# Laying r and k out with tokens along the row in a fused linear-attention and adapter-mixture kernel

## The chip, the cores and the metric

The kernel runs on one core of a Trainium2 chip. Five engines work side by side and meet at semaphores: TensorE (PE; its weight loads are listed as PEld), VectorE (DVE), ScalarE (ACT), GpSimd (POOL) and SyncE (SP, which here only issues DMAs). Matrix products land in PSUM, eight banks of 2 KB per partition; everything else lives in SBUF. The metric is the device time of one launch in microseconds, as a median over runs.

## The reference

Four batches of eight heads are run through a recurrence over 768 tokens with head size 48. Its output, seen as 3072 tokens of width 384, goes through a mixture of eight rank-16 adapters, of which each token takes the two with the largest gate logits.

```python
for t in range(S):                      # r, k, v, w: (4, 8, 768, 48); u: (8, 48)
    cur = np.einsum('bhd,bhe->bhde', u[None] * kt, vt)
    y[:, :, t] = np.einsum('bhd,bhde->bhe', rt, state + cur)
    state = wt[:, :, :, None] * state + np.einsum('bhd,bhe->bhde', kt, vt)
...
logits = x @ w_gate                     # x: y as (3072, 384)
topk = np.argpartition(-logits, K, axis=1)[:, :K]       # K = 2
...                                     # w: softmax over the two selected logits
delta[mask] += w[mask, k, None] * ((x[mask] @ A[e]) @ B[e])
return x + delta
```

## The kernel before, in words

The 3072 tokens are 24 tiles (`t`) of 128 tokens, six tiles per batch. A tile holds all eight heads, as four pairs `p` of two heads `g`, and everything below is done once per tile unless said otherwise.

- **Loads.** SP loads w (`load_w`) and v (`load_v`) in groups of one to three tiles, and r and k of one tile in one transfer (`load_rk`, 384 KB, eight buffers), all as f32 with tokens on the partitions and heads times 48 channels along the row. u and the adapter weights (`moe`) are loaded once.
- **Decay.** ACT takes the logarithm of w per group (`ln`). TensorE sums it over the tokens of the tile, and of the tile before, by triangular matrices into the bank `cs_ps`, in two steps: `csr` gives the sum before a token (it scales r), `csk` adds the token's own term (it scales k). ACT takes the exponentials (`expr`, `expk`) one after the other into a single bank `e_ps`, and DVE multiplies them onto r and k (`multr`, `multk`) into the bf16 tile `rk2`.
- **Turn.** TensorE transposes the eight 128-wide blocks of `rk2` (`trr`, `trk`) into `trp`, and ACT on even tiles, DVE on odd ones, copies them out (`trev`), so that channels are on the partitions.
- **Attention inside the tile.** TensorE multiplies turned k by turned r per head (`amm`, into `a_ps`, two banks); DVE applies the triangular mask to all 1024 columns at once (`aev`).
- **State.** TensorE accumulates k times v into the bank `s_ps` (`kv`), and ACT copies the sum to SBUF (`sev`). v comes as bf16 from a cast on ACT, per group (`vcast`).
- **Bonus, the u term.** POOL multiplies r by k (`rkk`) and by u (`rku`), DVE sums over the channels of each head (`diag`), POOL multiplies v by it (`dv`).
- **Output.** TensorE adds into `y_ps` the state's part and the bonus (`yin`) and the attention's part (`yat`); ACT copies it to SBUF (`xTev`).
- **Adapters.** TensorE computes logits into the same bank `s_ps` (`lg`); small instructions on ACT, DVE and POOL find the two largest (`lgs`, `gmax`, `gsel`, `gsub`, `gexp`, `gmul`, `gden`, `gnorm`); `zmm`, `zw`, `zT`, `zTev` apply A and the gate for three tiles at a time (one at the very end); `dx` and `dmm` add x and the product with B; ACT copies the result (`oev`) and SP stores it.

PSUM is handed out by name: one bank each for `cs_ps`, `s_ps`, `e_ps`, `trp`, `y_ps`, two for `a_ps`, and one (`m`) for the adapters, which near the end also borrow banks that are no longer used (`Z_BANK`, `D_BANK`).

The order of work is fixed: `ORDER` is one written list of task names, and each engine runs its own tasks in the order of that list. A planner class (`Plan`) holds the dependences and can make such a list from costs and priorities, but with `ORDER` present it only looks the tasks up. So an engine whose next task waits does not take a later one. Dependences that the list does not spell out are enforced by the framework, which adds the waits: two instructions that touch the same PSUM bank are kept in the order in which they are written.

Of the kernel before, what the change touches and what calls it, by code (L numbers as in the profile page):

```python
# [8 lines left out]
F32 = mybir.dt.float32  # L9
# [8 lines left out]
CENTRE = 52.0  # L18
# [5 lines left out]
    ld_u=-990.0,  # L24
    ld_v0=-985.0,
    ld_w1=-980.0,
    ld_rk1=-975.0,
    ld_rk2=-970.0,
    ld_v1=-965.0,
    ld_w2=-960.0,  # L30
    ld_rk3=-955.0,
    ld_rk4=-950.0,
    ld_rk5=-945.0,
    ld_v2=-940.0,
    ld_moe=-935.0,
    ld_w3=-930.0,
    ld_rk6=-925.0,
    ld_rk7=-920.0,
    ld_rk8=-915.0,
    ld_v3=-910.0,  # L40
    ld_w4=-905.0,
    ld_rk9=-900.0,
    ld_rk10=-895.0,
    ld_rk11=-890.0,
    ld_v4=-885.0,
    ld_w5=-880.0,
    ld_rk12=-875.0,
    ld_rk13=-870.0,
    ld_rk14=-865.0,
    ld_v5=-860.0,  # L50
    ld_w6=-855.0,
    ld_rk15=-850.0,
    ld_rk16=-845.0,
    ld_rk17=-840.0,
    ld_v6=-835.0,
    ld_w7=-830.0,
    ld_rk18=-825.0,
    ld_rk19=-820.0,
    ld_rk20=-815.0,
    ld_v7=-810.0,  # L60
    ld_w8=-805.0,
    ld_rk21=-800.0,
    ld_rk22=-795.0,
    ld_rk23=-790.0,
    ld_v8=-785.0,
    ln=17.78,
    csr=6.47,
    expr=-0.97,
    csk=0.14,
    multr=-14.6,  # L70
    expk=-5.95,
    multk=-9.66,
    rkk=10.33,
    rku=1.66,
    diag=6.67,
    dv=10.4,
    vcast=10.01,
    trr=13.31,
    trk=-10.55,
    trev=0.12,  # L80
    amm=10.34,
    aev=6.22,
    kv=-2.45,
    sev=11.79,
    yin=28.6,
    yat=-8.86,
    xTev=11.98,
    lg=15.76,
    dmm=8.44,
    oev=-6.55,  # L90
    store=0.0,
    lgs=5.8,
    gmax=-6.24,
    gsub=-4.6,
    gsel=-5.0,
    dx=5.0,
    gexp=5.87,
    gmul=7.19,
    gden=8.29,
    gnorm=-1.8,  # L100
    zmm=3.51,
    zw=-8.82,
    zT=-3.52,
    zTev=9.05,
# [11 lines left out]
consts ld_w0 ld_rk0 ln0 csr0 ld_v0 expr0 rkk0 ld_w1 csk0 multr0 vcast0 expk0 trr0 ld_u multk0 ln1 ld_rk1 kv0 rku0  # L116
csr1 trk0 sev0 expr1 ld_rk2 rkk1 trev0 csk1 multr1 diag0 ld_v1 expk1 amm0 csr2 trr1 multk1 rku1 dv0 rkk2 trk1 aev0
ld_w2 expr2 vcast1 yin0 csk2 multr2 trev1 rku2 expk2 kv1 yat0 ld_rk3 ln2 diag1 amm1 trr2 csr3 diag2 multk2 dv1
ld_rk4 aev1 sev1 xTev0 trk2 rkk3 expr3 ld_rk5 trev2 yin1 csk3 kv2 rku3 multr3 expk3 yat1 trr3 amm2 ld_v2 xTev1 diag3
multk3 csr4 dv2 rkk4 aev2 sev2 expr4 ld_moe rku4 rkk5 yin2 trk3 csk4 yat2 multr4 vcast2 trev3 expk4 ld_w3 kv3 xTev2  # L120
cast_wg multk4 dv3 rku5 sev3 trr4 csr5 diag4 trk4 expr5 amm3 trev4 multr5 ld_rk6 csk5 kv4 aev3 dv4 yin3 trr5 expk5
ln3 ld_rk7 rkk6 amm4 diag5 multk5 yat3 cast_A csr6 ld_rk8 aev4 xTev3 lg0 trk5 expr6 yin4 rku6 rkk7 dv5 cast_B ld_v3
multr6 csk6 trev5 expk6 sev4 lg1 yat4 xTev4 multk6 lg2 csr7 lg3 amm5 lg4 trr6 diag6 ld_w4 expr7 vcast3 rku7 rkk8
aev5 multr7 trk6 yin5 csk7 kv6 trev6 rku8 dv6 ld_rk9 yat5 diag7 expk7 amm6 ld_rk10 xTev5 multk7 rkk9 sev6 aev6 csr8
lg5 expr8 kv7 trr7 ld_rk11 lgs0 ln4 sev7 trk7 rkk10 gmax0 csk8 yin6 multr8 yat6 ld_v4 gsub0 gsel0 trev7 rku9 expk8
gexp0 csr9 multk8 xTev6 trr8 gmul0 diag8 dv7 expr9 trk8 ld_w5 gden0 trev8 amm7 kv8 lg6 multr9 gnorm0 csk9 yin7 aev7
expk9 sev8 zmm0 vcast4 dv8 rkk11 ld_rk12 multk9 csr10 zw0 yat7 amm8 expr10 diag9 ld_rk13 zT0 csk10 kv9 multr10 xTev7
rku10 rku11 dv9 rkk12 zTev0 yin8 trr9 trk9 expk10 aev8 ld_rk14 dmm0 ln5 csr11 multk10 ld_v5 oev0 yat8 trev9 sev9
expr11 dmm1 rku12 diag10 lg7 trr10 csk11 oev1 multr11 xTev8 ld_w6 diag11 expk11 trk10 dmm2 lg8 amm9 diag12 oev2
csr12 multk11 dv10 rkk13 dv11 trev10 aev9 ld_rk15 expr12 vcast5 multr12 zmm3 yin9 csk12 amm10 ld_rk16 zw3 yat9  # L130
expk12 aev10 rku13 rkk14 rku14 kv10 trr11 zT3 xTev9 ld_rk17 sev10 ln6 trk11 csr13 yin10 multk12 trev11 ld_v6 yat10
expr13 diag13 trr12 xTev10 trk12 diag14 rkk15 amm11 lg9 lg10 csk13 trev12 multr13 aev11 kv12 yin11 trr13 dv12 rku15
expk13 ld_w7 vcast6 csr14 multk13 yat11 zTev3 diag15 expr14 amm12 multr14 store2 ld_rk18 dmm3 trk13 csk14 xTev11
sev12 aev12 oev3 expk14 ld_rk19 store3 rkk16 dv13 rkk17 rku16 lg11 yin12 kv13 dmm4 csr15 multk14 yat12 trev13
ld_rk20 diag16 trr14 lgs1 ln7 expr15 sev13 multr15 xTev12 rku17 rkk18 amm13 csk15 trk14 gmax1 oev4 kv14 lg12 expk15
ld_v7 store4 gsub1 trev14 dv14 dmm5 yin13 csr16 gsel1 aev13 multk15 gexp1 yat13 sev14 diag17 gmul1 expr16 ld_w8 dv15
gden1 xTev13 amm14 trr15 trk15 csk16 kv15 multr16 oev5 gnorm1 lg13 yin14 aev14 dv16 rkk19 expk16 sev15 vcast7 zmm6
rku18 dv17 rkk20 multk16 ld_rk21 csr17 trev15 expr17 zw6 kv16 yat14 amm15 ld_rk22 multr17 csk17 zT6 trr16 trk16
# [725 lines left out]
```

## Time and profile before

| | |
|---|---|
| median of 3 runs | 102.93 us (102.78 to 103.38) |
| the profiled execution | 103.02 us, of which the span of the profile is 101.3 us |
| busy: PE, DVE, ACT, POOL | 85.6, 85.2, 80.5, 69.8 us (84%, 84%, 79%, 69% of the span) |
| weight loads (PEld) | 60.7 us |
| DMA | 24.5 MB, 9809 packets; the queue's packets took 64.5% of the 16 engines' span |
| granted TensorE clock | 0.989 of full speed |

Durations are those of one profiled execution. Records overlap: eight matmuls of L460 have 222 ns each and are over in 0.40 us, and on DVE a mask multiplication recorded with 1.22 us is followed by the next instruction after 1.13 us. Where the time that an instruction holds its engine is wanted, the chain of waits is read, in which pieces follow one another without overlap.

### The profile page before, as it was taken

How to read it: one execution, taken by the hardware profiler on the slowest of the kernel's cores; microseconds unless marked ns; L12 is line 12 of the kernel's file. 1: busy time of each engine (PE TensorE's matmuls, PEld its weight loads, DVE VectorE, ACT ScalarE, POOL GpSimd, SP SyncE). 2: the span in 40 equal slices, each digit the busy share in tenths (PEclk: the TensorE clock that was granted, in tenths of full speed). 3: DMA queues.
4: the chain of work that ended last, by engine and by line, in shares of the span. 5: the costliest groups of instructions: out<-in, count | busy, mean ns of one | idle time of the engine just before them, and what ended most of it. 6: DMA issues, size and time to landing. Idle time of an engine off the chain costs nothing.

```text
span 101.3 us, 3568 instructions
## 1 busy us (share of the span) xinstructions
PE 85.6 (84%) x1400; PEld 60.7 (60%) x1400; DVE 85.2 (84%) x203; ACT 80.5 (79%) x160; POOL 69.8 (69%) x93
## 2 busy tenths in 40 slices
PE   1238899998698699999999999999988999999930
PEld 0014556566476477677766686678765777778620
DVE  4723898989978899999999899899969898988920
ACT  5347589999699898999999898798995678764640
POOL 6317989999999889999999989999972400000000
PEclk9999999999999999999999999999999999999995
DMA  2899999999999976948006989961224003224173
GB/s 55 298 312 400 414 421 422 409 417 413 428 398 422 416 258 209 385 149 283 11 0 194 377 283 312 382 250 66 100 82 154 6 32 126 84 78 155 40 292 140
DMA packets 9809, 24.50 MB, mean 242 GB/s; under 512 B 1088, under 2 KB 4544, under 8 KB 9792
## 3 DMA queue, kind: packets, MB, share of 16 engines
q1 hardware_dynamic: 9792, 24.27, 64.5%
q8 instruction: 11, 0.18, 0.7%
q14 instruction: 6, 0.05, 0.1%
HBM read 19.55 MB, written 4.72 MB: 240 GB/s over the span
## 4 chain that ended last, share of the span: by engine, by line
PE 54%; DVE 22%; ACT 7%; DMA 5%; issue 4%; POOL 3%; SPq 1%; ACTq 1%; DVEq 0%
DVE at L466 8%; PE y_ps L508 6%; PE a_ps L460 6%; PE y_ps L499 5%; PE y_ps L494 5%; DMA v_in<-in_v_dram 5%; PE trp L438 4%; PE z_ps L601 4%; PE d_ps L640 4%; PE trp L443 3%; DVE rk L414 3%; DVE rkT L449 3%; PE s_ps L476 3%; PE cs_ps L388 3%; PE s_ps L519 3%
## 5 line engine op out<-in xcount | busy, mean ns | idle before, releaser
L466 DVE TENSOR_TENSOR at<-a_ps,at_mask 128x1024 bf16<-128x1024 f32 x24 | 29.3, 1219 | 1.4 <-PE a_ps L460 1.3
L422 POOL TENSOR_TENSOR rku<-rku,u_sb 128x384 f32<-128x384 f32 x24 | 23.9, 1000 | 3.4 <-DMA u_sb<-in_u_dram 2.6
L418 POOL TENSOR_TENSOR rku<-rk_in 128x384 f32<-128x384 f32 x24 | 23.9, 998 | 1.7 <-DMA rk_in<-in_rk_dram 1.7
L431 POOL TENSOR_TENSOR dv<-v_in,diag 128x384 bf16<-128x384 f32 x24 | 19.8, 830 | 0.2 <-DVE diag L426 0.2
L514 ACT CAST xT<-y_ps 128x512 bf16<-128x512 f32 x24 | 14.3, 598 | 2.0 <-PE y_ps L508 1.9
L398 ACT ACTIVATE e_ps<-cs_ps 128x384 f32<-128x384 f32 x24 | 11.7, 486 | 5.1 <-PE cs_ps L390 2.5
L409 DVE TENSOR_TENSOR rk<-rk_in,e_ps 128x384 bf16<-128x384 f32 x24 | 13.2, 548 | 2.9 <-ACT e_ps L398 2.9
L414 DVE TENSOR_TENSOR rk<-rk_in,e_ps 128x384 bf16<-128x384 f32 x24 | 13.2, 549 | 2.6 <-ACT e_ps L403 2.5
L403 ACT ACTIVATE e_ps<-cs_ps 128x384 f32<-128x384 f32 x24 | 11.8, 493 | 2.2 <-PE cs_ps L393 1.2
L426 DVE TENSOR_REDUCE diag<-rku 128x8 f32<-128x384 f32 x24 | 12.8, 548 | 0.3 <-POOL rku L422 0.3
L651 ACT COPY res<-d_ps 128x384 f32<-128x384 f32 x22 | 10.6, 486 | 2.6 <-PE d_ps L647 2.1
L451 ACT COPY rkT<-trp 128x1024 bf16<-128x1024 bf16 x12 | 12.3, 1026 | 0.0
L379 ACT CAST v_bf<-v_in 128x1152 bf16<-128x1152 f32 (+2 forms) x9 | 9.4, 1048 | 1.6 <-DMA v_in<-in_v_dram 1.6
L438 PE MATMUL trp<-ident,rk 128*128 128x128 bf16 x96 | 9.8, 227 | 1.0 <-DVE rkT L449 0.7
L373 ACT ACTIVATE logw<-w_in 128x1152 f16<-128x1152 f32 (+2 forms) x9 | 9.6, 1061 | 1.3 <-DMA w_in<-in_w_dram 1.2
L460 PE MATMUL a_ps<-rkT 48*128 48x128 bf16 x192 | 9.8, 222 | 0.9 <-ACT rkT L451 0.7
L390 PE MATMUL cs_ps<-logw,strict 128*128 128x384 f16 x24 | 8.4, 349 | 2.1 <-ACT logw L373 2.1
L508 PE MATMUL y_ps<-at,v_bf 128*64 128x128 bf16 x192 | 9.8, 224 | 0.2
L443 PE MATMUL trp<-ident,rk 128*128 128x128 bf16 x96 | 9.8, 227 | 0.1
L499 PE MATMUL y_ps<-ident,dv 128*128 128x128 bf16 x96 | 9.7, 225 | 0.0
L438 PEld LDWEIGHTS <-rk 128*128 128x128 bf16 x96 | 6.5, 101 | 4.3 <-DVE rk L409 1.5
L393 PE MATMUL cs_ps<-logw,ident 128*128 128x384 f16 x24 | 8.3, 348 | 0.7 <-ACT e_ps L398 0.6
(71 smaller groups left out, 160.8 us busy)
## 6 DMA issues: line engine op xcount, KB each, us to landing
rk_in<-in_rk_dram SPq DMA_DIRECT2D x24, 384.0 KB, 7.2
out_dram<-res SPq DMA_DIRECT2D x24, 192.0 KB, 1.9
w_in<-in_w_dram SPq DMA_DIRECT2D x7, 576.0 KB, 8.3
v_in<-in_v_dram SPq DMA_DIRECT2D x7, 576.0 KB, 8.4
moe_f<-in_moe_dram SPq DMA_DIRECT2D x1, 464.0 KB, 8.7
w_in<-in_w_dram SPq DMA_DIRECT2D x1, 384.0 KB, 5.2
v_in<-in_v_dram SPq DMA_DIRECT2D x1, 384.0 KB, 6.9
w_in<-in_w_dram SPq DMA_DIRECT2D x1, 192.0 KB, 2.4
```

The costliest lines, as they stand in the source:

```text
L409: nc.vector.tensor_mul(rk2[:, 0].rearrange("s p h d -> s (p h) d")[:, :, 0:D], chunk(t, "r"), st[t]["er"])
L414: nc.vector.tensor_mul(rk2[:, 1].rearrange("s p h d -> s (p h) d")[:, :, 0:D], chunk(t, "k"), st[t]["ek"])
L418: nc.gpsimd.tensor_mul(rku, chunk(t, "r"), chunk(t, "k"))
L422: nc.gpsimd.tensor_mul(st[t]["rku"], st[t]["rku"], u_sb)
L431: nc.gpsimd.tensor_mul(dv_[:, :, 0:D], chunk(t, "v"), st[t]["diag"].to_broadcast([L, H, D]))
L438: nc.tensor.transpose(trp[:, 0, p, :], st[t]["rk2"][:, 0, p, :, :].rearrange("s a b -> s (a b)"), ident)
L443: nc.tensor.transpose(st[t]["trp"][:, 1, p, :], st[t]["rk2"][:, 1, p, :, :].rearrange("s a b -> s (a b)"), ident)
L460: nc.tensor.matmul(a_ps[:, g, p, :], lhsT=rkT[base:base + D, 1, p, :], rhs=rkT[base:base + D, 0, p, :], start=True, stop=True)
L466: nc.vector.tensor_mul(at, st[t]["a_ps"].rearrange("s g p f -> s (g p) f"), at_mask.to_broadcast([128, H, 128]))
L499: nc.tensor.matmul(y_ps[:, p, :], lhsT=dv_[:, 2 * p:2 * p + 2, :].rearrange("s a b -> s (a b)"), rhs=ident, start=(c == 0 and p == 0), sto ...
L508: nc.tensor.matmul(y_ps[g * 64:(g + 1) * 64, p, :], lhsT=vb[:, 2 * p + g, :], rhs=at[:, g * P + p, :], start=False, stop=(p == P - 1), ski ...
L514: nc.scalar.copy(out=xT_, in_=st[t]["y_ps"])
```

## The change

r and k come from the host with channels on the partitions and tokens along the row (head pairs padded from 48 to 64 channels, so a tile is 512 KB; after the eight buffers have been filled once, 112 of 128 partitions, 448 KB). The log sums are made in that shape, with logw as the stationary operand and the triangular matrix moving, once per tile (`cs`) in place of the two steps; the sum before a token is the sum up to the token before it, so r is multiplied by the exponential shifted by one column (`multr`) and its first column by the last column of the tile before (`rz`). Scaled r and k are then already turned: `trr`, `trk`, `trev` are gone, and only k is transposed back for the state (`ktr`, `knev`; not in the last tile of a batch). The constant that centres the exponents moves from a matmul into the bias of the exponentials. The bonus is one product on POOL and a sum on TensorE against a block form of u (`rkk`, `bon`, into a further part of `s_ps`), copied out by ACT (`diag`). v is padded to 64 per head on the host and cast to bf16 by its DMA, which POOL issues; so are the adapter weights with u. `vcast`, the three `cast_` tasks, `rku` and the load of u are gone. `aev` is two instructions, one per bank. Except for `cs_ps` and `s_ps`, PSUM is one pool of six banks: a task that takes a bank gets the one that has been free longest in the written order. `ORDER` is written anew, with `PRIO` and the planner's costs.

The parts of the diff that do the work (`PRIO`, `ORDER`, the planner's costs and the removed functions, which stand above, are left out):

```diff
     def load_v(gi):
-        nc.sync.dma_start(out=g["v"][:, 0:g["n"]], in_=v[:, g["t0"]:g["t0"] + g["n"]])
+        g["v"] = ld.tile([L, GN, H, DP], BF16, name="v_bf", bufs=NV)
+        nc.gpsimd.dma_start(out=g["v"][:, 0:g["n"]], in_=v[:, g["t0"]:g["t0"] + g["n"]])
     def load_rk(t):
+        st[t]["rk"] = rk_ins[t % NRKI]
+        rows = 128 if t < NRKI else 64 + D
+        nc.sync.dma_start(out=st[t]["rk"][0:rows], in_=rk[0:rows, t])
+    def load_moe():
+        nc.gpsimd.dma_start(out=moe_bf, in_=moe)
...
+    def bank(key, shape, dt):
+        taken[key] = idle.pop(0)
+        return pp.tile(shape, dt, name=f"bk{taken[key]}", tag=f"bk{taken[key]}")
+    def release(key):
+        idle.append(taken.pop(key))
...
+    def cs(t):
         c = t % NC
+        for p in range(P):
+            if c > 0:
+                nc.tensor.matmul(cs_ps[:, p, :], lhsT=pair_of(grp(t - 1, "logw"), p), rhs=rest, start=False,
+                                 stop=False, skip_group_check=True)
+            nc.tensor.matmul(cs_ps[:, p, :], lhsT=pair_of(grp(t, "logw"), p), rhs=incl, start=(c == 0 and p == 0),
+                             stop=True, skip_group_check=True)
+    def expr(t):
+        e = bank(f"er{t}", [128, P, 128], F32)
+        nc.scalar.activation(out=e, in_=cs_ps, func=ACT.Exp, bias=up)
+    def expk(t):
+        e = bank(f"ek{t}", [128, P, 128], F32)
+        nc.scalar.activation(out=e, in_=cs_ps, func=ACT.Exp, bias=down, scale=-1.0)
+    def multr(t):
+        nc.vector.tensor_mul(st[t]["rT"][:, :, 1:128], st[t]["rk"][:, 0, :, 1:128], st[t]["er"][:, :, 0:127])
+    def rz(t):
+        if t % NC == 0:
+            nc.gpsimd.memset(rTs[t % NRT][:, :, 0:1], 0.0)
         else:
+            nc.vector.tensor_mul(rTs[t % NRT][:, :, 0:1], st[t]["rk"][:, 0, :, 0:1], st[t - 1]["er"][:, :, 127:128])
     def multk(t):
+        nc.vector.tensor_mul(st[t]["kT"], st[t]["rk"][:, 1], st[t]["ek"])
     def rkk(t):
+        x = wk.tile([128, P, 128], BF16, name="rkx", bufs=3)
+        nc.gpsimd.tensor_mul(x, st[t]["rk"][:, 0], st[t]["rk"][:, 1])
+    def bon(t):
+        for p in range(P):
+            nc.tensor.matmul(dg_ps[:, t % NSL, :], lhsT=st[t]["rkx"][:, p, :], rhs=u_bf[:, p, :],
+                             start=False, stop=(p == P - 1), skip_group_check=True)
     def diag(t):
-        nc.vector.tensor_reduce(out=dg, in_=st[t]["rku"], axis=AX.X, op=ALU.add)
+        nc.scalar.copy(out=dg.rearrange("s h o -> s (h o)"), in_=dg_ps[:, t % NSL, :])
+    def ktr(t):
+        kn_ps = bank(f"kn{t}", [L, P, 128], BF16)
         for p in range(P):
+            nc.tensor.transpose(kn_ps[:, p, :], st[t]["kT"][:, p, :], ident)
+    def knev(t):
+        x = st[t]["kn_ps"].rearrange("s p (g d) -> s (p g) d", g=2)[:, :, 0:D]
+        if knev_on_dve(t):                                # odd tiles
+            nc.vector.tensor_copy(out=kn, in_=x)
         else:
+            nc.scalar.copy(out=kn, in_=x)
+    def amm(t, g):                                        # one bank per call, all eight matmuls in the second
+        st[t]["a_ps", g] = bank(f"a{g}_{t}", [128, P, 128], F32)
...
+    def aev(t, i):
+        at = wk.tile([128, 4, 128], BF16, name=f"at{i}")
+        nc.vector.tensor_mul(at, st[t]["a_ps", i], at_mask.to_broadcast([128, 4, 128]))
```

The new list begins so:

```
consts ld_moe ld_w0 ld_rk0 ln0 cs0 ld_w1 expk0 rkk0 expr0 multk0 ld_rk1 ln1 multr0 rz0 ld_v0 bon0 ktr0 diag0 cs1
ld_rk2 knev0 rz1 amma0 ammb0 rkk1 expk1 aevb0 expr1 ld_w2 multk1 cs2 rkk2 multr1 ktr1 expk2 bon1 aeva0 diag1 expr2
dv0 bon2 ld_rk3 rz2 amma1 ln2 kv0 ammb1 ld_v1 knev1 multk2 yin0 multr2 yat0 ld_rk4 sev0 cs3 rz3 diag2 aevb1 rkk3
```

## The prediction, made before the changed kernel was run

> **What bounds the kernel now.** I read the busy shares by stage first.
>
> ```profile
> 10.00:35.00 25.00, 21.28 (x336) 14.62 (x335) 22.63 (x43) 21.91 (x43) 24.11 (x29) 1.00 1.03 416
> 35.00:62.00 27.00, 26.59 (x476) 19.21 (x476) 26.54 (x54) 25.95 (x51) 25.68 (x32) 1.00 0.67 224
> 62.00:95.00 33.00, 31.73 (x552) 23.84 (x547) 29.86 (x76) 25.00 (x53) 15.19 (x20) 1.00 0.35 128
> ```
>
> The columns are the stretch, then busy us of PE, PEld, DVE, ACT and POOL, the clock, the DMA share and GB/s. No engine is alone at its limit: POOL is full up to 35 us (24.11 of 25), PE and DVE are at 98% up to 62 us, and afterwards PE leads (31.73 of 33) while POOL runs dry. DMA is full only in the first stretch. Then the chain that ended last, by engine:
>
> ```profile
> PE 54%; DVE 22%; ACT 7%; DMA 5%; issue 4%; POOL 3%; SPq 1%; ACTq 1%; DVEq 0%
> ```
>
> So PE sets 54.7 us of the 101.3 and DVE 22.3. The same chain in order of time shows what an instruction holds its engine when the next stands right behind it (start, length):
>
> ```profile
> 56.66 1.13 DVE at L466
> 57.79 0.46 DVE rk L414
> 58.25 0.46 DVE diag L426
> ...
> 68.11 0.33 PE a_ps L460 x8
> 68.44 0.33 PE trp L438 x4
> 69.10 0.22 PE trp L443 x4
> ```
>
> 1024 columns hold DVE 1.13 us and 384 hold it 0.46, which is 1.05 ns a column; four 128-wide transposes with their weight loads hold PE 0.22. For ACT and POOL I use the costliest groups (busy, mean ns, idle before):
>
> ```profile
> L422 POOL TENSOR_TENSOR rku<-rku,u_sb 128x384 f32<-128x384 f32 x24 | 23.9, 1000 | 3.4 <-DMA u_sb<-in_u_dram 2.6
> L418 POOL TENSOR_TENSOR rku<-rk_in 128x384 f32<-128x384 f32 x24 | 23.9, 998 | 1.7 <-DMA rk_in<-in_rk_dram 1.7
> L514 ACT CAST xT<-y_ps 128x512 bf16<-128x512 f32 x24 | 14.3, 598 | 2.0 <-PE y_ps L508 1.9
> L451 ACT COPY rkT<-trp 128x1024 bf16<-128x1024 bf16 x12 | 12.3, 1026 | 0.0
> L379 ACT CAST v_bf<-v_in 128x1152 bf16<-128x1152 f32 (+2 forms) x9 | 9.4, 1048 | 1.6 <-DMA v_in<-in_v_dram 1.6
> ```
>
> Last, two waits. One is at the start, a row of the timeline (the bracket is idle time before it):
>
> ```profile
> 6.40 0.51 ACT L379 CAST v_bf<-v_in 128x384 bf16<-128x384 f32 x1 [1.56 <-DMA v_in<-in_v_dram]
> ```
>
> The other is in the list of waits (total us, times, longest):
>
> ```profile
> PE s_ps L519 <- ACT S_sb L482: 1.5, 3, 0.9
> ```
>
> The first cast of v stands ahead of the first `expk` in ACT's order, so the start hangs on v. And `lg` waits for ACT's reading of other columns of `s_ps`: whoever uses that bank is kept in the written order.
>
> **The change, part by part.**
>
> *PE, per tile.* Before, by chain pieces and distances in the timeline: `csr` and `csk` 3 x 0.16 = 0.48, `trr` and `trk` 0.44, `amm` 0.33, `kv` 0.24 x 20/24 = 0.20, `yin` 0.34 x 20/24 + 0.33 = 0.61, `yat` 0.34, `lg` 0.11, `zmm` 0.67/3 = 0.22, `zT` 0.27/3 = 0.09, `dx` and `dmm` 0.34: together 3.16. The first 0.92 go. New: `cs`, eight matmuls of 128 columns each with its own weights, like eight transposes 0.44 (four in the first tile of a batch, mean 0.40); `ktr` 0.22 x 20/24 = 0.18; `bon`, four matmuls of 8 columns like `lg`, 0.11. That is 0.69, so 0.23 less a tile, 7.3%, 5.5 us over 24 tiles.
>
> *DVE, per tile.* Before 1.13 + 3 x 0.46 + 0.61/2 (`trev` on odd tiles) = 2.81. New: two masks of 512 columns, 0.59 each; `multk` 0.59 and `multr` (508) 0.59; `rz`, four columns, between 0.05 by the slope and 0.16 by the 8-column rows, taken as 0.08 x 20/24 = 0.07; `knev` on eight tiles, 384 bf16 columns from PSUM, 0.27 like `zTev` (0.46 if the gaps in its source cost it that), x 8/24 = 0.09. Sum 2.52: 0.29 less, 6.9 us over 24 tiles. Splitting and widening cost DVE, the bonus sum and the turned copies leaving it gain more.
>
> *ACT.* Gone: L379 9.4, L451 12.3 and the three casts of the adapter weights 0.62 + 0.51 + 0.23, together 23.1. Added: 512 for 384 columns in 48 exponentials, 598 against about 490 ns, 5.2; `knev` on twelve tiles, 486 ns as `oev` with 384 columns, 5.8; `diag` 24 x 0.2 (the row with 48 columns takes 198 ns), 4.8. Net 7.3 less of 80.5, 9%.
>
> *POOL.* L418 and L422 go, 47.8. The new product has 512 columns: from 998 ns at 384 and about 275 at 48 columns it is 1.27 us; writing bf16 could make it 1.11 (830 x 4/3 from `dv`). 24 x 1.27 = 30.5. Ten DMA issues come onto POOL's queue; no DMA of POOL's is in this trace, so I bound one by SP's 0.33 us and by a POOL product, 1.0, and take 1.0, as POOL is the engine that computes: 10 us. What is queued behind an issue is the next `rkk` or `dv`. Net 7 us less, and POOL had room in the last stretch already; it stops being what the first 35 us wait for. On the chain it has 3%, counted as nothing.
>
> *DMA.* r and k: 8 x 512 + 16 x 448 KB against 24 x 384, v 24 x 256 against 24 x 192, u gone, moe 16 KB more: 24.3 becomes 27.8 MB, 74% for 64.5% of the engines. In steady state a tile needs 0.98 MB, 2.4 us at 416 GB/s, against 3.4 us a tile now (first `yat` at 13.7, last at 92.7 us, 23 steps): hidden. If the pace fell under 2.4 us it would not be.
>
> *The start.* `vcast` no longer blocks ACT, but PE's new order is `cs0 bon0 ktr0 cs1 amma0`, so everything on PE now stands behind `bon0`, which waits for `rkk0` and for the adapter load that carries u. POOL's masks end at 2.9 us; a load issued then took 2.4 us at best (first w), 8.7 at worst (moe itself, behind a full queue); u, issued at 2.65, was waited for until 8.2. I take 5.5, landing at 8.4; PE got to `kv0` at 7.9 before, and `amm0`, at 10.6 then, no longer waits for a transpose and a 1.0 us copy. The first `yin` needs `rkk2` and `dv0` on POOL, so 2.9 MB, which the rates of the first stages (176, 352, 418 GB/s) give at 10.6 us; plus 1.27 + 0.83 it is 12.7, against 12.6. Net zero, between 1.5 us sooner and 3.2 later. The page "DMA: Bandwidth & Descriptors" of the Trainium skill (Issuing engine by pattern, and Specifications) speaks against this part: loads issued by GpSimd are generally the slower ones, with a first byte after about 1 us against 0.6; by that the start and the sum would be 0.4 us later, an estimate from that page, and no run so far shows it.
>
> *PSUM.* Waits that lose their ground: `expk` and `expr` for the multiplication before (0.8 + 0.4), transposes for the copy (0.7 + 0.7), `amm` for the mask (0.3). These are 2.9 us, of which the transposes' 0.7 is listed for PE and again for its weight load, so 2.2 at most; another wait may stand behind each, so zero is taken. Against that, `s_ps` gets one more writer (`bon`) and reader (`diag`) a tile. Its waits now are 1.5 (`lg` for `sev`), 1.1 and 0.2 (`sev` for `kv`, `lg`): 2.8 us in 44 visits of PE. 24 more visits make 1.5, half of it on the path: 0.8 us lost.
>
> *Sum.* PE's part of the chain 54.7 x 7.3% = 4.0; DVE's 22.3 x 6.9/79.0 (its busy time from 10 to 95 us) = 1.9; ACT's 7.1 x 9% = 0.6; less 0.8: 5.7 us. The two full engines taken alone say 5.5 and 6.9, so the sum doesn't hang on how the chain is shared out. From the profiled execution's 103.02 (span 101.3 and 1.7 around it) it is 97.3, and as the median lies 0.1 lower, 97.2 us.
>
> **The rivals.**
>
> *The bank `s_ps` becomes the handover that everyone stands in (slower).* PE may write `kv` or `lg` only when ACT has read `diag`, and `diag` stands in ACT's strict order behind exponentials of 0.6 us. Each exposed wait costs what the three listed ones cost, 1.5/3 = 0.5 us; one in every tile is 12 us, of which 0.8 is counted: 108.4 us. It decides from 5.7/24 = 0.24 us a tile on. For it: PE leads the last third, and the new list often puts `lg` or `kv` right behind a `bon`. Against it: 21 of 24 `lg` now pass without such a wait. The page "PSUM — Partial Sum Buffer" of the Trainium skill (PSUM bank collisions raise a hardware error) has the rule that PSUM be guarded by bank, not by address; the row of `lg` waiting for `sev` agrees, with 0.9 us at the longest.
>
> *The adapter load comes late.* At the upper bound, 8.7 us, it lands at 11.6 and all of PE starts 3.2 us later: 100.4 us. For it: it is issued behind a queue that SP has filled. Against it: u did better there.
>
> *The gain turns into waiting.* All four engines get lighter together, yet tiles advance by cross-engine handovers in a fixed list; if those set the pace, the time stays: 103 us. Against it: in the middle stretch PE, DVE and ACT are busy 96% or more, and the path of a tile loses a transpose and a copy.
>
> **How the numbers follow.** Forecast 97.2, chance 0.59, with 94.0 (start 1.0 sooner, 2.2 of PSUM waits gone) to 99.5 (`rkk`, `rz`, `knev` and part of the start at their upper ends). Late load 0.13, gain lost 0.05, `s_ps` 0.23, since the waits there are few now but the change adds to just these. Half a per cent, 0.5 us, is about what a measurement can tell. Faster 0.59 + 0.13 = 0.72, same 0.05, slower 0.23. The range runs from 94.0 to 105.0; above it is the greater part of the `s_ps` case.
>
> **What would show it.** Right: DVE's records fall by some 6 us, ACT's by 7, POOL's products by 17; L379, L451 and both transposes of r are gone; PE's chain share stays the largest; `yin` starts near 12.7 us. Wrong: waits of `kv`, `lg` or `bon` for `diag` over 5 us in total; PE idle until 11 us behind `bon`; new products on POOL over 1.4 us, or DMA issues there over 1 us, so that `dv` holds `yin`; eight-matmul groups of `cs` over 0.5 us.

## The result: 11% slower, and the profile after

The changed kernel took 114.2 to 114.9 us where the kernel before takes 103.1: a ratio of 1.111 (1.103 to 1.120). All ratios are against the kernel before on the same chip. All times below are those of a version's shortest executions, within 1.5% of its best; the longer ones, in the versions of the change often the majority, partly at full granted clock and for no reason that is shown, are left out, but several traces below and the medians in some expectations are of them. A single number is one execution.

The work of DVE, ACT and POOL came out lighter, as forecast. The page of the changed kernel, its busy times:

```profile
PE 89.8 (79%) x1488; PEld 70.7 (62%) x1488; DVE 78.5 (69%) x215; ACT 75.9 (67%) x172; POOL 59.1 (52%) x83
```

DVE fell from 85.2 to 78.5, ACT from 80.5 to 75.9, POOL from 69.8 to 59.1. PE, forecast to fall by 5.5, rose from 85.6 to 89.8, as equal matmuls took longer (those of `yat` 258 ns on average against 224; more on this below). What grew most is waiting. The chain that ended last, by engine and then by line, against PE 54%, DVE 22%, DMA 5% before:

```profile
DMA 39%; PE 37%; DVE 6%; POOL 6%; issue 4%; ACT 3%; SPq 0%; POOLq 0%; ACTq 0%; DVEq 0%
DMA v_bf<-in_v_dram 35%; PE bk L495 4%; PE bk L503 4%; PE bk L490 4%; PE bk L585 4%; PE bk L460 4%; DMA rk_in<-in_rk_dram 3%; POOL dv L436 3%; PE bk L621 3%; POOL rkx L421 2%; DVE at L465 2%; PE bk L628 2%; PE cs_ps L390 2%; PE bk L442 2%; PE cs_ps L392 2%
```

A third of the span is one kind of transfer, the v loads that the change gave to POOL. Read in order of time, the same chain shows how they hang together (start, length):

```profile
6.32 7.08 DMA v_bf<-in_v_dram
13.53 0.75 POOL dv L436
14.30 6.98 DMA v_bf<-in_v_dram
21.41 0.77 POOL dv L436
22.18 9.35 DMA v_bf<-in_v_dram
...
41.90 0.56 POOL dv L436
42.67 7.59 DMA v_bf<-in_v_dram
```

A load, the multiplication that waits for it, the issue of the next load, seven us of landing, the next multiplication. The instructions of POOL show why (start, length, and in the bracket the idle time before):

```profile
13.53 0.83 POOL L436 TENSOR_TENSOR dv<-v_bf,diag 128x384 bf16<-128x384 bf16 x1 [1.86 <-DMA v_bf<-in_v_dram]
14.30 0.59 POOL L306 DMA_DIRECT2D v_bf<-in_v_dram  x1
14.91 2.50 POOL L421 TENSOR_TENSOR rkx<-rk_in 128x512 bf16<-128x512 f32 x2
21.41 0.83 POOL L436 TENSOR_TENSOR dv<-v_bf,diag 128x384 bf16<-128x384 bf16 x1 [4.00 <-DMA v_bf<-in_v_dram]
22.18 0.59 POOL L306 DMA_DIRECT2D v_bf<-in_v_dram  x1
```

`ld_v1` stands behind `dv0` in the written list, and `dv0` waits for `ld_v0`. All four v buffers are free then, so nothing else holds the issue. The seven us of one landing are no property of POOL's loads alone, as SP's took as long in this kernel (KB each, median us from issue to landing); but SP has nothing to compute and issues its loads ahead:

```profile
rk_in<-in_rk_dram SPq DMA_DIRECT2D x16, 448.0 KB, 8.1
rk_in<-in_rk_dram SPq DMA_DIRECT2D x8, 512.0 KB, 10.9
v_bf<-in_v_dram POOLq DMA_DIRECT2D x7, 384.0 KB, 7.6
moe_bf<-in_moe_dram POOLq DMA_DIRECT2D x1, 240.0 KB, 8.5
```

The list of waits (total, times, longest) has the cost, a wait that is new and one that was 1.7 before:

```profile
POOL dv L436 <- DMA v_bf<-in_v_dram: 18.3, 5, 6.2
PE s_ps L426 <- DMA moe_bf<-in_moe_dram: 7.0, 1, 7.0
POOL rkx L421 <- DMA rk_in<-in_rk_dram: 6.7, 4, 2.9
```

And the stretch of the steady loads, columns as in the prediction (PE, PEld, DVE, ACT, POOL, clock, DMA share, GB/s):

```profile
20.00:50.00 30.00, 26.85 (x436) 20.42 (x433) 22.62 (x51) 21.93 (x48) 16.82 (x19) 1.00 1.04 270
```

The transfer engines are full (1.04) but move 270 GB/s; before they moved 416 at a share of 1.03. The view counts a casting load by the bytes that it writes, half of what it reads: the 1.2 MB that they wrote here make it some 310 GB/s by bytes read, still far under 416. This is the second new thing, and no part of the prediction had it.

To see where the time went, the span is cut at the identity matmuls of the first and the last tile's `yin`. The rows of that line: durations as min/median/max ns, then the starts of the first and the last; before, then after.

```profile
L499 PE MATMUL y_ps<-ident,dv x96: 216/219/314, 12.6 to 91.8; 128*128 128x128 bf16 x96
L495 PE MATMUL bk<-ident,dv x96: 216/229/314, 17.3 to 104.5; 128*128 128x128 bf16 x96
```

| | start, to the first `yin` | steady, to the last | tail |
|---|---|---|---|
| before (span 101.3) | 12.6 | 79.2 | 9.5 |
| forecast (95.6) | 12.7 | 73.4 | 9.5 |
| after (113.2) | 17.3 | 87.2 | 8.7 |

The forecast's steady part is what its start and an unchanged tail leave of its span. The miss of 17.6 us is 4.6 in the start and 13.8 in the steady part, less 0.8 in the tail.

### The profile page after: what moved, and what is told of

Read it like the earlier page. It is cut to its first block, busy times and chain, and to the rows that moved or that the text cites. A ratio compares the mean times of both kernels' runs of the same rounds, so it can differ in the third digit from the quotient of the medians.

```text
span 113.2 us, 3740 instructions
## 1 busy us (share of the span) xinstructions
PE 89.8 (79%) x1488; PEld 70.7 (62%) x1488; DVE 78.5 (69%) x215; ACT 75.9 (67%) x172; POOL 59.1 (52%) x83
## 4 chain that ended last, share of the span: by engine, by line
DMA 39%; PE 37%; DVE 6%; POOL 6%; issue 4%; ACT 3%; SPq 0%; POOLq 0%; ACTq 0%; DVEq 0%
DMA v_bf<-in_v_dram 35%; PE bk L495 4%; PE bk L503 4%; PE bk L490 4%; PE bk L585 4%; PE bk L460 4%; DMA rk_in<-in_rk_dram 3%; POOL dv L436 3%; PE bk L621 3%; POOL rkx L421 2%; DVE at L465 2%; PE bk L628 2%; PE cs_ps L390 2%; PE bk L442 2%; PE cs_ps L392 2%
## 5 line engine op out<-in xcount | busy, mean ns | idle before, releaser
L465 DVE TENSOR_TENSOR at<-bk,at_mask 128x512 bf16<-128x512 f32 x48 | 31.7, 683 | 11.8 <-PE bk L460 11.1
L421 POOL TENSOR_TENSOR rkx<-rk_in 128x512 bf16<-128x512 f32 x24 | 30.1, 1265 | 6.8 <-DMA rk_in<-in_rk_dram 6.7
L436 POOL TENSOR_TENSOR dv<-v_bf,diag 128x384 bf16<-128x384 bf16 x24 | 19.8, 828 | 24.0 <-DMA v_bf<-in_v_dram 18.3
L417 DVE TENSOR_TENSOR kT<-rk_in,bk 128x512 bf16<-128x512 f32 x24 | 16.3, 681 | 5.8 <-ACT bk L402 5.6
L509 ACT CAST xT<-bk 128x512 bf16<-128x512 f32 x24 | 14.4, 600 | 7.1 <-PE bk L503 7.1
L392 PE MATMUL cs_ps<-incl,logw 128*128 128x128 f16 x96 | 16.0, 255 | 3.9 <-ACT logw L381 3.9
L402 ACT ACTIVATE bk<-cs_ps,down 128x512 f32<-128x512 f32 x24 | 16.1, 669 | 3.6 <-PE cs_ps L392 2.0
L397 ACT ACTIVATE bk<-cs_ps,up 128x512 f32<-128x512 f32 x24 | 16.0, 666 | 3.2 <-PE cs_ps L392 3.2
L407 DVE TENSOR_TENSOR rT<-rk_in,bk 128x508 bf16<-128x508 f32 x24 | 16.2, 675 | 1.8 <-ACT bk L397 1.8
L392 PEld LDWEIGHTS <-logw 128*128 128x128 f16 x96 | 10.3, 114 | 5.1 <-ACT logw L381 3.9
L426 PEld LDWEIGHTS <-rkx 128*128 128x128 bf16 x96 | 4.9, 101 | 10.6 <-issue 9.8
L495 PE MATMUL bk<-ident,dv 128*128 128x128 bf16 x96 | 11.4, 254 | 0.0
L390 PEld LDWEIGHTS <-logw 128*128 128x128 f16 x80 | 8.9, 114 | 1.2 <-issue 0.7
```

What stands on the lines that cost most here:

```text
L390: nc.tensor.matmul(cs_ps[:, p, :], lhsT=pair_of(grp(t - 1, "logw"), p), rhs=rest, start=False, stop=False, skip_group_check=True)
L392: nc.tensor.matmul(cs_ps[:, p, :], lhsT=pair_of(grp(t, "logw"), p), rhs=incl, start=(c == 0 and p == 0), stop=True, skip_group_check=True)
L397: nc.scalar.activation(out=e, in_=cs_ps, func=ACT.Exp, bias=up)
L402: nc.scalar.activation(out=e, in_=cs_ps, func=ACT.Exp, bias=down, scale=-1.0)
L407: nc.vector.tensor_mul(st[t]["rT"][:, :, 1:128], st[t]["rk"][:, 0, :, 1:128], st[t]["er"][:, :, 0:127])
L417: nc.vector.tensor_mul(st[t]["kT"], st[t]["rk"][:, 1], st[t]["ek"])
```

## The experiments

**The v loads issued early.** Theory A was that the place of the v loads in POOL's queue makes the loss; its rival B, that transfers through POOL are slow or the whole change is. Only the list changes:

```diff
-consts ld_moe ld_w0 ld_rk0 ln0 cs0 ld_w1 expk0 rkk0 expr0 multk0 ld_rk1 ... rkk1 ... rkk2 ...
+consts ld_moe ld_v0 ld_w0 ld_rk0 ln0 cs0 ld_w1 expk0 rkk0 ld_v1 expr0 ... rkk1 ld_v2 ... rkk2 ld_v3 ...
```

Each later load stands behind the first product or multiplication on POOL that follows the last reader of its buffer.

> The changed kernel with its loads of v issued sooner on POOL (the first right behind the adapter load, the next three behind the first three products, the rest as soon as their buffer is free), nothing else moved. Theory A (issue: each load of v stands in POOL's order behind a dv that waits for the load before, so loads of 7 to 9 us follow one another): the waits of dv for v fall from 18 us to under 5 and the time to 104 to 107 us. Theory B (service: the casting loads themselves are slow and the DMA engines are full, whenever they are issued): little changes, 111 to 115 us. Theory C (the bank s_ps or the bank pool paces the kernel): nothing changes, 113 to 115 us.

Measured: 105.3 to 106.2 us, ratio 1.027 (1.019 to 1.035), as theory A had it, and under what B and C had. The row of the identity matmuls, and two rows of its waits:

```profile
L495 PE MATMUL bk<-ident,dv x96: 216/219/314, 17.1 to 95.1; 128*128 128x128 bf16 x96
POOL dv L436 <- DMA v_bf<-in_v_dram: 1.2, 1, 1.2
POOL rkx L421 <- DMA rk_in<-in_rk_dram: 7.4, 6, 3.0
```

`dv` waits 1.2 us for v instead of 18.3, the steady part is 78.0 instead of 87.2, and the start is where it was. So 9 of the 17.6 us were the issue order. It is still not faster than before, and the wait for r and k remains.

**v without POOL's transfers.** v comes as f32 through SP, where it was before, and a cast on ACT:

```diff
-        nc.gpsimd.dma_start(out=g["v"][:, 0:g["n"]], in_=v[:, g["t0"]:g["t0"] + g["n"]])
+        nc.sync.dma_start(out=g["v_in"][:, 0:g["n"]], in_=v[:, g["t0"]:g["t0"] + g["n"]])
...
+        nc.scalar.copy(out=g["v"][:, 0:g["n"], :, 0:D], in_=g["v_in"][:, 0:g["n"]])
```

> The changed kernel with the v part undone: v without padding as f32 by SP in line with the loads of r and k, cast on ACT, POOL issues only the adapter load. Theories A and B both: no wait for v is left, 96 to 101 us if the rest of the change is worth what was forecast (7 us of ACT's gain go back). Theory C: still over 108 us.

Measured: 111.5 to 112.5 us, ratio 1.088 (1.079 to 1.097). Theories A and B missed by over 10 us. By its number this is on C's side, but its waits in `s_ps` for `diag` come to 1.3 us in all, so its trace does not bear C out. Its stages:

```profile
10.00:20.00 10.00, 7.37 (x90) 6.14 (x92) 5.27 (x11) 6.45 (x14) 5.27 (x6) 1.00 1.03 419
20.00:50.00 30.00, 26.81 (x490) 20.53 (x485) 24.53 (x55) 26.84 (x59) 18.05 (x22) 0.99 1.03 298
```

With no transfer of POOL's in flight but the adapters', SP's queue moves 419 GB/s while the 512 KB loads of the first eight tiles run, and 298 afterwards, when the 448 KB loads of 112 rows run, with the engines full in both. Theory D came from these two lines: the loads of 112 partitions are the slow ones. Another part of the miss is my list: `dv` waits 10.3 us for the casts, which I had set too late.

**The v load alone, in the kernel before.** One part of the change alone: the padded v and its cast by POOL's DMA, at the places where SP issued v.

> The kernel before with only one part of the change: v padded to 64 and cast by a DMA that POOL issues, at the places of the list where SP's loads of v stood, which is well ahead of use; no cast on ACT. Theory A: no loss from it, 100 to 104 us (ACT is 9 us lighter, POOL, which is full, 5 us heavier). Theory B: the loads come late here too, 106 us or more, with waits of dv or kv for v above 5 us.

Measured: 111.6 to 112.0 us, ratio 1.086 (1.076 to 1.096). By its number, and by its waits for v of 6.7 us (`dv`) and 10.1 us (`kv`), this is B's side. Its trace showed the mechanism of A as well: POOL, with two products a tile, reached the third issue only at 20.1 us and the fourth at 34.4, though the list had them as early as SP's were, and `dv` and `kv` waited for the landings. So this run alone does not tell the two theories apart; the early issues above do, and the loads by themselves, below, say how far B holds.

**The bonus later on PE.** `bon0` and its reader go behind the attention of tile 0, so that nothing of PE stands behind the adapter load.

```diff
-... rz0 ld_v0 bon0 ktr0 diag0 cs1 ... amma0 ammb0 rkk1 ...
+... rz0 ld_v0 ktr0 cs1 ... amma0 ammb0 bon0 diag0 rkk1 ...
```

> The changed kernel with only the first bonus sum moved on PE, from ahead of the first attention product to behind it, so that PE does not stand at bon0 for the adapter load until 11.5 us. Theory A or B: the first dv waits for v anyhow, so at most 1 us is won, 113.5 to 115 us. The rival of the late adapter load as a cause by itself: 3 us or more are won, 111 us or less.

Measured: 112.1 and 113.2 us, ratio 1.095 (1.083 to 1.107); 1 to 3 us less than the changed kernel, between the two expectations. In its trace the first `yin` starts at 15.3 us, not 17.3, and `dv` still waits 16.2 us for v. The late load costs a little while v is late, and is not the loss.

**All 128 rows**, on the changed kernel, on the one with early v loads, and on the one with v through SP:

```diff
-        rows = 128 if t < NRKI else 64 + D
-        nc.sync.dma_start(out=st[t]["rk"][0:rows], in_=rk[0:rows, t])
+        nc.sync.dma_start(out=st[t]["rk"], in_=rk[:, t])
```

> The changed kernel with one number changed: r and k of the tiles from the ninth on are loaded with all 128 rows (512 KB) instead of the 112 that hold data (448 KB), so 1.0 MB more is read. Theory D (loads of 112 rows move at 260 to 300 GB/s where loads of 128 rows moved at 420, and the transfers are full until 50 us): the stretches from 20 to 50 us rise to about 400 GB/s; the chain still runs over the v loads that GpSimd issues late, so 108 to 113 us. Theory A alone (only the place of the v issues in GpSimd's queue matters): 114 to 116 us, the same as before or 1 us worse for the added bytes.

> The changed kernel with both edits: the v loads issued early on GpSimd, and all 128 rows of r and k loaded. Theory A with D: the v waits are gone and the transfers run at about 400 GB/s instead of 270, so the wait of GpSimd's products for r and k (7.4 us in the run with the early issues alone) mostly goes: 98 to 102 us. A without D: 105 to 107 us, nothing gained over the early issues alone (105.8).

> v as f32 through the SP queue with its cast on ScalarE, and all 128 rows of r and k loaded. Theory D: the run with v through SP (112.1 us) missed its forecast because the 112-row loads ran at 260 to 345 GB/s from 20 us on; with 128 rows 97 to 103 us, and no stretch under 390 GB/s before 40 us. Rival (the transfers are slow because more is in flight at once, whatever the rows): 110 to 113 us.

Measured: 107.9 and 108.7 us, ratio 1.050 (1.041 to 1.060); 100.3 and 100.9, ratio 0.978 (0.970 to 0.985); and 110.3, ratio 1.099 (1.089 to 1.109). Reading 1.0 MB more made the changed kernel some 6 us faster and the one with early loads 5 us; with both edits the change is 2.2% under the kernel before, at the edge of what the runs tell apart. D holds in these two. The third missed its time but shows the rate most plainly, as nothing else differs from the run with v through SP:

```profile
20.00:35.00 15.00, 13.70 (x236) 10.51 (x233) 12.32 (x25) 12.82 (x27) 8.91 (x11) 1.00 1.03 417
```

417 GB/s in place of 298. It lost the gain to my list: `dv` still waited 10.6 us for the casts, and SP, whose next task was a store, waited 17.8 us for ACT with the loads of later tiles behind it.

**The loads by themselves.** A kernel of loads only, whose r and k loads go through SP as before; each phase waits for the one before, and the stores of its zeros start behind the last r, k load.

> A kernel of loads alone: it computes nothing of the reference and stores zeros. One after the other, each waiting for the one before: six r, k loads of 128 rows (4 KB each), of 112, of 128 again, of 120, of 96, of 64 and 48 rows in two transfers; three v loads with the cast; six loads of 128 rows beside three v loads; six of 112 beside three v loads; one load of 128 rows; one of 112; one v load. Theory D (the number of rows sets the rate): 128 rows at about 420 GB/s, which is 7.5 us for six; 112 rows at 340 GB/s or less, so that 448 KB take longer than 512 KB. If row count is innocent, 112 rows take 7/8 of the time of 128. The v loads alone, if their 7 to 9 us are made by the busy queue: 3 us for one; if by the kind of transfer: 6 us or more for one.

VectorE reads one element of each load in turn, so its idle times are the distances of the landings. First four loads of 112 rows, then four of 128, then three v loads in a row; last SP's stores (row of its queue) and the single v load that ran beside them:

```profile
18.46 0.14 DVE L45 COPY seen<-rk_in 1x1 f32<-1x1 f32 x1 [4.05 <-DMA rk_in<-in_rk_dram]
20.15 0.14 DVE L45 COPY seen<-rk_in 1x1 f32<-1x1 f32 x1 [1.55 <-DMA rk_in<-in_rk_dram]
21.85 0.14 DVE L45 COPY seen<-rk_in 1x1 f32<-1x1 f32 x1 [1.55 <-DMA rk_in<-in_rk_dram]
23.52 0.14 DVE L45 COPY seen<-rk_in 1x1 f32<-1x1 f32 x1 [1.53 <-DMA rk_in<-in_rk_dram]
...
30.77 0.14 DVE L45 COPY seen<-rk_in 1x1 f32<-1x1 f32 x1 [3.46 <-DMA rk_in<-in_rk_dram]
32.06 0.14 DVE L45 COPY seen<-rk_in 1x1 f32<-1x1 f32 x1 [1.15 <-DMA rk_in<-in_rk_dram]
33.51 0.14 DVE L45 COPY seen<-rk_in 1x1 f32<-1x1 f32 x1 [1.31 <-DMA rk_in<-in_rk_dram]
34.79 0.14 DVE L45 COPY seen<-rk_in 1x1 f32<-1x1 f32 x1 [1.14 <-DMA rk_in<-in_rk_dram]
...
83.46 0.14 DVE L45 CAST seen<-v_bf 1x1 f32<-1x1 bf16 x1 [5.00 <-DMA v_bf<-in_v_dram]
85.27 0.14 DVE L45 CAST seen<-v_bf 1x1 f32<-1x1 bf16 x1 [1.68 <-DMA v_bf<-in_v_dram]
87.12 0.14 DVE L45 CAST seen<-v_bf 1x1 f32<-1x1 bf16 x1 [1.71 <-DMA v_bf<-in_v_dram]
...
125.18 15.86 SPq L85 DMA_DIRECT2D out_dram<-res  x24
137.63 0.14 DVE L45 CAST seen<-v_bf 1x1 f32<-1x1 bf16 x1 [7.78 <-DMA v_bf<-in_v_dram]
```

From the first to the fifth landing of a phase, per load:

| rows | KB | us apart | GB/s |
|---|---|---|---|
| 128 | 512 | 1.33 | 396 |
| 120 | 480 | 2.05 | 240 |
| 112 | 448 | 1.69 | 272 |
| 64 and 48, two transfers | 448 | 1.95 | 235 |
| 96 | 384 | 1.48 | 266 |

D is shown without the kernel around it, in one run: leaving out 16 rows of 128 makes the load 27% longer. Two phases mix the kinds: six loads of 128 rows beside three v loads took 15.3 us from the first issue on POOL to the last landing, six of 112 rows beside three v loads 15.5. So there the 0.4 MB less brought nothing, but cost next to nothing either.

The first v load of the three landed 4.7 us after its issue (78.6 to 83.4) with no load or store of SP's in flight, between the 3 and the 6 us of the expectation. The two behind it followed, 1.8 us apart (768 KB read each, 430 GB/s). A load of 512 KB by SP alone took some 3.6 (issued at 120.8, read at 124.5). Beside other transfers the same v load took longer: 7.5 and 8.0 us for the first one beside SP's loads, 7.5 for the single one, which shares the engines with the stores of the zeros. So POOL's transfers are not slow at several in a row, and some 3 of the 7 to 8 us that one takes to land in the changed kernel (7.6 in the median, less 4.7) come from the company of others. This speaks for theory A, which needs a long landing and a late issue, and against B, which has the loads slow whenever they are issued. The page "DMA: Bandwidth & Descriptors" of the Trainium skill (Rules for kernel authors) asks for 128 partitions, and at least 1 MiB a transfer, for the highest bandwidth; of the row counts in the table, at half a MiB, 128 was the fastest.

**u ahead, and loads ahead of stores.** Both start from the kernel with early v loads and 128 rows. First, the adapter load is split: u, 8 KB of bf16, goes first of POOL's loads, and the rest behind the third v load. Then, in addition, the r, k loads 18 to 21 stand ahead of the first store in SP's queue, and 22, 23 and the last w ahead of the third.

```diff
+        nc.gpsimd.dma_start(out=moe_bf[:, U0:], in_=moe[:, U0:])
...
-... ld_w7 store1 ld_rk18 store0 ld_rk19 store3 ld_rk20 ld_w8 ...
+... ld_w7 ld_rk18 ld_rk19 ld_rk20 ld_rk21 store1 store0 ld_rk22 ld_w8 ld_rk23 store3 ...
```

> The changed kernel with early v issues and 128 rows (103.5 us), and the adapter load split: its last columns, which hold u, as a transfer of their own ahead of all of GpSimd's others, the rest behind the third v load. TensorE's wait of 6.8 us for that load, 7.1 us of it in order ahead of other work, is to go to under 2 us: 98 to 101 us if the late adapter load is a cost once v is in time; 102 to 104 if the start is bound by something else (the row loads, the logs).

> As the run with u first, and in SP's queue the r, k loads of tiles 18 to 23 and the last w load stand ahead of the stores that they were queued behind (a store waited 13.8 us for its tile with the load of tile 18 behind it, and GpSimd then waited 4.0 us for that load). If that queue order costs: 1 to 4 us less than the run with u first. If the wait is covered: within 0.5 us of it.

Measured: 100.4 us for the first, nothing gained. The row of its load in the second kernel (KB, us to landing) says why:

```profile
moe_bf<-in_moe_dram POOLq DMA_DIRECT2D x1, 8.0 KB, 7.7
```

8 KB took nearly as long to land as the 384 KB of a v load, 8.5 us in this trace; in the run with few rows, below, it was 6.6. With the loads ahead of the stores: 98.7 to 99.6 us, ratio 0.962 (0.957 to 0.966). That is 1 to 2 us less, and the best version that was run, under both kernels; below it is called the mended version.

**u, and the first v, through SP**, on the mended version, with a cast of u on DVE and of the first tile's v on ACT (the v loads behind it move up in POOL's order):

```diff
-        nc.gpsimd.dma_start(out=moe_bf[:, U0:], in_=moe[:, U0:])
+        nc.sync.dma_start(out=u_f, in_=moe[:, U0:])
...
+        if gi == 0:
+            nc.sync.dma_start(out=v0_in, in_=v[:, 0])
```

> As the run with the row loads ahead of the stores (99.6 us), with u alone moved off GpSimd: 16 KB as f32 through SP's queue behind the first r, k load, cast on VectorE (about 0.1 us). GpSimd's transfer of 8 KB for the same columns took 7.7 us to land, and TensorE waited 6.2 us for it. If the landing of a GpSimd transfer is what holds the start: the first bonus sum runs at about 7 us instead of 10.7, TensorE's wait for it goes, 96 to 98.5 us. If v of the first tile (landed at 12.7) is the next bound at the same place: 98.5 to 99.6.

> As the run with u through SP, and v of the first group (one tile, 256 KB) also through SP as f32 with its cast on ScalarE (0.65 us), so that only the later groups depend on GpSimd's transfers. If the landing of v of the first tile is the next bound: the first multiplication of the difference into the output at 10 us instead of 14 or so, and 1 to 3 us under the run with u alone. If not (the second tile's v, or the logs, come last): within 0.7 us of it.

Measured: 100.5 us, and 99.8 and 100.7 (ratio 0.973, 0.967 to 0.979). The wait for u falls from 6.2 us to 2.1 and 2.4 in the traces, and the first `yin` of the second starts at 15.4 us instead of 16.5, but no time is gained: the first missed its expectation, and the second came out on the side on which the first tile's v is not the next bound.

**TensorE kept busy at the start.** In all versions of the change whose start was not filled, the eight matmuls of `yat` take some 80 ns each at first, in most up to 25 us and beyond, and mostly 51 ns afterwards; before they take some 50 from the first on. The rows for `yat` from 25 to 40 us (PE's busy us and number of matmuls first, then PEld, clock, DMA share, GB/s), before and after:

```profile
25.00:40.00 15.00, 1.64 (x32) 1.02 (x32) 1.00 0.92 355
25.00:40.00 15.00, 1.92 (x24) 1.20 (x24) 1.00 1.05 275
```

That is 51 and 80 ns each. Matmuls that nobody reads fill PE's idle start:

```diff
+            for i in range(n):
+                nc.tensor.matmul(w_ps, lhsT=incl, rhs=incl, start=True, stop=True)
```

60 of them on the mended version and on the changed kernel as it is; 12 and 28, and then 12, 28, 30, 18 and 12 in five places, on the version with u and the first v through SP.

> As the run with the row loads ahead of the stores (99.6 us), with 60 matmuls of 128 x 128 by a constant, whose result nobody reads, on TensorE behind the first log sum, in the 6 us in which it waits for u. If TensorE's slow start is a cause of its own: the output's matmuls take 51 ns instead of 80 from 15 us on, some 15 us of dense work at 80 ns shrink by up to a third, 95 to 97.5 us, and the runs spread less. If the slow matmuls only follow from late data: 99 to 100 us, nothing gained.

> The changed kernel as it is, with the same 60 matmuls behind the first log sum. The chain of v loads behind GpSimd's multiplies sets its time up to 40 us, so by theory A the faster TensorE has nothing to do earlier and gains at most 2 us: 112 to 116. If TensorE's slow start were the main cause of the loss: under 108.

> As the run with u and the first v through SP (102.9 us median, 99.8 at best), with 12 such matmuls ahead of the first log sum and 28 behind it. If the slow start is the cause and the early data then count too: 94 to 97 us, under the run with the 60 matmuls. If the early data are worth nothing even so: the same as that run. If the slow matmuls only follow from late data: 99.5 to 103.

> As the run with 40 such matmuls, u and the first v through SP (100.4 us at best), with 30, 18 and 12 more of these matmuls where TensorE waited 1.8, 1.2 and 0.8 us between 7.9 and 14.3 us. If its slow start is the rest of the loss: the output's matmuls at 51 ns from 15 us on and 95 to 98 us, under both kernels and under the mended version. If the early time is worth nothing because something else (the row loads, GpSimd's products) sets the pace: 99 to 101.

Measured: 99.3 to 100.6 us (ratio 0.969, 0.962 to 0.976); 114.4 and 115.2 (1.113, 1.104 to 1.122); 100.4 and 100.5 (0.974, 0.967 to 0.981); and 99.0. In the trace of the first, `yat` runs at 51 ns from its first tile up to 25 us, and nothing is gained, though there the clock falls later (0.50 from 45 to 50 us, with 80 ns again); the last came nearest to the mended version and not under its best. The slow start is real, but making it fast gained no time in any of the four.

**Fewer bytes.** The mended version with only 16 of 128 rows of r and k loaded from tile 8 on, 7.3 MB less (the other rows keep old data, so that part of the input is left out); and, with the data kept, the version with u through SP with all of v as unpadded f32 through SP, read by POOL as it is and cast on ACT.

> As the run with the row loads ahead of the stores (99.6 us), but the r, k loads of tiles 8 to 23 bring only 16 of the 128 rows (64 KB; the other rows keep the values of eight tiles before), so that 7.3 MB less is read. If the transfers, full until 62 us, are what holds the mended version over the forecast: 93 to 97 us, and the waits of GpSimd's products for r, k gone. If they are covered and the engines set the time: 98.5 to 99.6.

> As the run with u through SP (100.5 us at best), with all of v through SP as unpadded f32 (0.19 MB a tile instead of 0.26), the difference's multiply on GpSimd reading that f32 tile, and the cast of v for TensorE on ScalarE (some 0.4 us a tile, 9 us in all, which ScalarE at 76 of 100 us has room for). If GpSimd's transfers (7 to 9 us to land, padded bytes) are the rest of the loss: the transfers done by 55 us and 95 to 98 us. If ScalarE's added casts take it back: 99 to 102. If the order of the loads in the one queue starves one input again, as in the first run with v through SP: over 104.

Measured: 100.3 us and 103.6 us. Emptying the transfers brought nothing, so, as far as one execution shows it, they do not set the mended version's time. The second paid for its casts and its longer SP queue. The identity matmuls of two runs, the one with 40 filling matmuls and the one with few rows:

```profile
L520 PE MATMUL bk<-ident,dv x96: 216/220/315, 15.7 to 89.8; 128*128 128x128 bf16 x96
L500 PE MATMUL bk<-ident,dv x96: 216/219/314, 15.4 to 89.8; 128*128 128x128 bf16 x96
```

Two different reliefs end in the same steady part, 74.1 and 74.4 us, one us over the forecast's 73.4. What is left is the start: 15.4 us against 12.7. The run with few rows starts like the mended version, its r, k loads being the same up to tile 7, and has its first `yin` at 15.4 without u or v through SP; so it is not shown that moving them brought the 15.4 of the run above.

## Why the prediction was wrong, step by step

- **DVE** was right: 6.9 us less forecast, 6.7 measured. The masks and products of 512 columns hold it as sized, and so do `knev` and `rz`.
- **POOL's products** were right to the digit (1.27 us forecast, 1265 ns measured), and an issue of a load holds POOL 0.59 us, inside the bounds of 0.33 and 1.0.
- **ACT** was mis-sized: 4.6 us less instead of 7.3. The exponentials of 512 columns take 666 and 669 ns, not 598, which is 3.3 us over 48; `diag` at 177 ns gave 0.6 back.
- **PE's pace** was not met in the changed kernel: its busy time rose by 4.2 us where 5.5 less were forecast, and at first the eight matmuls of `cs` ran 0.107 us apart, 0.86 us a group, a sign of being wrong that the prediction had named (over 0.5). It can be read only in later versions: in the run with few rows PE is busy 81.8 us, 3.8 less than before, and the steady part of 74.1 to 74.4 us stands for the whole chain sum (5.7 us forecast; 79.2 less 74.1 is 5.1). So the sum of the engines was right within a us there; that the changed kernel would reach it with its data in time is argued from those runs, not measured.
- **"What is queued behind an issue is the next `rkk` or `dv`"** is the step that failed most, and with it "On the chain it has 3%, counted as nothing". The prediction asked who waits behind an issue on POOL and not what the issue itself waits behind. The list it had shown has `dv0` ahead of `ld_v1` and `kv0 ... ld_v1 ... yin0`; a load that lands 7 us after its issue and is issued behind the user of the load before makes a serial chain. It had no term for this; issuing early took 9 us off.
- **"2.4 us at 416 GB/s against 3.4 us a tile: hidden"** failed by its rate. From the loads alone, a tile of 112 rows takes 1.69 us, its share of a v load 0.61, and its w (196,608 bytes at 396 GB/s) 0.50: 2.8 us, and 3.3 with a store at the same rate, an estimate, against a forecast pace of 73.4/23 = 3.2. Its 0.98 MB a tile is short too: 448 KB of r and k, 256 of v, 192 of w and 192 stored are 1.11 MB. The prediction counted the 64 KB left out as a saving; they cost 5 to 6 us. Why fewer rows are slower, no run shows.
- **The start** failed by its landing: the adapter load landed at 11.4 us, close to the upper bound of 11.6 and not at 8.4, so that PE stood until 11.5 behind `bon`, another sign of being wrong that the prediction had named; v of the first tile landed at 13.4, and the first `yin` came at 17.3 instead of 12.7. The data of `rkk2` were in time (its product ran from 10.4 us). With both landings made early, the first `yin` still starts at 15.4, so the sum of 12.7 missed something else on that path that no run isolated.
- **PSUM and `s_ps`** were right: `bon` waits 0.6 us in total for `diag`, `lg` and `kv` 0.5. The rival with 0.5 us a tile is dead. The rival of the late adapter load met its condition (11.4) and not its price: it had 3.2 us, but with `bon` out of the way the changed kernel gained 1 to 3, and with u through SP the mended one nothing.
- **The page cited for POOL's loads** ("DMA: Bandwidth & Descriptors" of the Trainium skill, Issuing engine by pattern, and Specifications) had the right sign, and the 0.4 us estimated from it is about what the loads alone show: 4.7 us against 3.6 for SP's, of which 0.6 is an estimate for the 256 KB more that it reads, at 430 GB/s. What the start paid is the landing among other transfers, 8.5 us for the adapter load, where SP's first load had taken 2.4.

What stays open: the mended version's 1.5 to 2.4 us over the forecast belong mostly to the start, if the cut of the span of those two runs holds for it, but making u, v and TensorE's clock early one after the other left the first `yin` at 14.9 us or later and the time where it was. A version with few rows and a filled start at once was not run.

## What to carry to other kernels

Before a load is given to an engine that computes, look at what stands ahead of its issue in that engine's order: if it is a user of the load before, the two are serial, and the landing, which the other transfers stretch, is paid once for each. Fewer bytes are not less transfer: price a load by its shape, from a run with that shape and with the same company in flight. A forecast of engine work is worth only as much as the check that each input is there when the lighter engines ask for it, so cut the span at the first and the last use of a late input and give each piece a number.

## What the hardware did that was not expected

- Loads of 4 KB rows to 112, 120 or 96 partitions moved 272, 240 and 266 GB/s, those to 128 moved 396; in the kernels with v through SP 298 against 417, with the transfer engines shown full in both. Beside three casting loads, six loads of 112 rows took 15.5 us and six of 128 rows 15.3.
- A transfer issued by GpSimd that casts (384 KB written) landed 4.7 us after its issue with no load or store of SP's in flight, 7.5 to 8.0 beside loads or stores of SP, and with a median of 7.6 in the changed kernel and 9.9 with early issues; several in a row followed 1.8 us apart. With queues busy, 8 KB took 6.6 and 7.7 us.
- TensorE ran slow although it was dense: in the changed kernel `yat`'s matmuls took 80 ns from 15 to 40 us, with PE busy 9.6 of 10 us from 20 to 30, while the clock column said 1.00. In the run with 40 filling matmuls the same 80 ns stand from 15 to 25 us with 0.5 in the clock column. So at the start of a span the clock column alone doesn't tell; equal matmuls compared over time do. The page "TensorE: Matmul & The Clock Gate" of the Trainium skill (Part 1: The HAM clock gate) says that about 4 us of steady matmuls release the clock. The filled idle start agrees with it (matmuls of the log sums 0.06 us apart behind it instead of 0.11); the stretch from 20 to 30 us, dense by its busy share, does not.
